# Loading and norming two heads first, and no weight product between the first head's scores

## The chip, the cores and the metric

The kernel runs on one core of a Trainium2 chip. Its time is device microseconds (us) of one execution. Three runs of the kernel before gave 1234.19 us as the median (1233.05 to 1234.97). One further execution was taken by the hardware profiler and took 1230.67 us, with a span of 1228.6 us from the first to the last instruction.

The engines are PE (matrix products), DVE (vector), ACT (scalar, with the exponentials), POOL (GpSimd) and SP, which here issues nearly all DMAs. Each works through its own instructions in order and waits for the others by semaphores.

## The reference

Four batches of attention with 12 heads, 448 rows and head width 64, on normed queries and keys, are followed by two dense blocks. All arrays are float32, except the weights of the dense blocks, which come as float64.

```
rmsnorm(x, g) = x / sqrt(mean(x*x, -1) + 1e-6) * g
scores = (1/8) * rmsnorm(q, g_q) @ rmsnorm(k, g_k).T
attn = softmax(scores);  x = attn @ v            # heads side by side: [1792, 768]
x = relu(x @ moe_w_in)**2 @ moe_w_out            # 768 -> 2048 -> 768
out = (((x @ w1) * (x @ w2)) @ w3) @ moe2_w_out  # 768 -> 1024 -> 1024 -> 768
```

The kernel uses that the last two products need no value between them: it forms W3O = w3 @ moe2_w_out once, at the start, and multiplies by that.

## The kernel before, in words

**Precision.** A product is made of three matmuls: each operand is split into a high part, which the matmul takes without loss, and a low part (the rest), and `mm3` (L260) adds high by high, high by low and low by high. L262, L263 and L264 are these three.

**Weight units.** The weights arrive as `units`: 128 partitions by 384 or 512 columns. A unit in float64 passes five steps: a load by SP (L180) into one of four `raw64` buffers; `words` (L191), where ACT rescales the upper word (L194) and POOL, for one unit in three ACT (L198), takes 16 bits of the lower word (L200); `join` on DVE (L207) makes a float32 and frees the load's buffer; `split_hi` on ACT (L106) makes the high part, and `split_lo` (L114) the low part, on POOL for four units in five and on DVE for the fifth. `advance` (L240) runs these steps some units ahead of use. The first 18 units, counted here from 0, belong to W3O: unit 0 (w3), 1 to 4 (wo), 5 (w3), 6 to 17 (wo). Unit 18 is the w3 unit of the second row of W3O, and from there on no wo unit is needed.

**W3O.** `gen_w3o` (L272) makes W3O in 8 rows of 48 matmuls, 384 in all. It and, for a batch later, `gen_moe` are generators: `fill(n)` (L649) lets the current one issue about n matmuls between stages of the attention. W3O's matmuls are recorded between the stages of heads 0 to 12, the dense blocks of batch 0 between those of heads 13 to 24, and so on.

**Heads.** `load_group` (L390) loads queries and keys of four heads for the norms, `load_head` the transposed queries of one head, `load_v` its values. `group_prep` (L438) squares them on ACT (L451), sums on DVE (L453), and makes 1/rms (L428 to L435, two steps of it on ACT); `sums` and `norm` of the first group are called in parts. `head_prep` (L475) scales the keys on POOL (L481), splits them (L108, L114: `khl`) and splits the queries (L492, L497). `stage_k` transposes the keys on PE (L509: `kv`) and copies them (`kt`). `stage_qk` makes the scores of two of a head's four 112-row chunks (L525, L526: `sc`, two PSUM buffers) and their maxima (L527, L528: `nb`). `stage_exp` takes the exponentials on ACT (L544: `p`). `stage_t` transposes the probabilities on PE (L571: `pt`), `stage_v` multiplies them by the values (L623).

**The order.** The program records instructions in the order of the loop at the end (L678). A scheduling layer then sets the order on each engine: it may place an instruction ahead of earlier ones that it expects to be still waiting. On the chip each engine keeps that order.

Of the kernel before, what the change touches and what calls it, by code (L numbers as in the profile page):

```python
# [29 lines left out]
def attention_moe_kernel(  # L30
# [15 lines left out]
    nc = tc.nc  # L46
    B, P, H, C, D = q_nat.shape
    S = P * C
    NH = B * H
    GH = 4  # L50
# [120 lines left out]
    def is64(i):  # L171
        return units[i][0].dtype != F32

    def load_next():
        i = pos["load"]
        src = units[i][0]
        n = src.shape[-1]
        if is64(i):
            t = t3.tile([128, 512, 2], U32, name="raw64", tag="raw64", bufs=4)
            nc.sync.dma_start(out=t[:, :n, :], in_=src.bitcast(U32).rearrange("p (n t) -> p n t", t=2))  # L180
        else:
            t = rawp.tile([128, 512], F32, name="raw", tag="raw")
            nc.sync.dma_start(out=t[:, :n], in_=src)
        raws[i] = t
        pos["load"] += 1

    def load_to(i):
        while pos["load"] <= min(i, NU - 1) and is64(pos["load"]):
            load_next()
# [200 lines left out]
    def load_group(g):  # L390
        if not (0 <= g < NH // GH):
            return
        b, h0 = divmod(g * GH, H)
        qn = t1.tile([P, GH, C, D], F32, name="qn", tag="qn")
        kn = t2.tile([P, GH, C, D], F32, name="kn", tag="kn")
        if g == 0:
            nc.sync.dma_start(out=kn[:, 0:1], in_=k_nat[0, :, 0:1])
            load_head(0)
            nc.sync.dma_start(out=qn[:, 0:1], in_=q_nat[0, :, 0:1])
            load_to(0)  # L400
            nc.sync.dma_start(out=kn[:, 1:], in_=k_nat[0, :, 1:GH])
            nc.sync.dma_start(out=qn[:, 1:], in_=q_nat[0, :, 1:GH])
            load_to(1)
        else:
            nc.sync.dma_start(out=kn, in_=k_nat[b, :, h0:h0 + GH])
            nc.sync.dma_start(out=qn, in_=q_nat[b, :, h0:h0 + GH])
        grp[g] = [qn, kn, None, None]

    def load_head(h):
        if not (0 <= h < NH):  # L410
            return
        b, hh = divmod(h, H)
        t = t2.tile([128, S], F32, name="qt", tag="qt")
        nc.sync.dma_start(out=t, in_=q_t[b, hh])
        qts[h] = t
# [9 lines left out]
    def rsqrt(y, x):  # L425
        t = small.tile([P, 2, GH * C], F32, name="nt", tag="nt")
        t = t[:, :x.shape[1], :x.shape[2]]
        nc.vector.tensor_scalar(  # L428
            out=y.bitcast(I32), in0=x.bitcast(I32), scalar1=-0.5, scalar2=1597463007.0, op0=ALU.mult, op1=ALU.add
        )  # L430
        nc.vector.tensor_tensor(out=t, in0=y, in1=y, op=ALU.mult)
        nc.vector.tensor_tensor(out=t, in0=t, in1=x, op=ALU.mult)
        nc.scalar.activation(out=t, in_=t, func=AF.Ln)
        nc.scalar.activation(out=t, in_=t, func=AF.Exp, scale=-0.5)
        ins = nc.vector.tensor_tensor(out=y, in0=t, in1=y, op=ALU.mult)  # L435
        return ins.ins

    def group_prep(g):  # L438
        if not (0 <= g < NH // GH):
            return  # L440
        qn, kn = grp[g][:2]
        n = GH * C
        if g == 0:
            sq = hlp.tile([128, 1024], F32, name="sq", tag="hl")[:P].rearrange("p (h c d) -> p h c d", h=GH, c=C)
        else:
            sq = qn
        ss = small.tile([P, 2, n], F32, name="ss", tag="ss")
        rr = grp[g][2] = t2.tile([P, 2, n], F32, name="rr", tag="rr")

        def sums(i, x, sq, a, b):  # L450
            nc.scalar.activation(out=sq[:, a:b], in_=x[:, a:b], func=AF.Square)  # L451
            t = sq[:, a:b].rearrange("p h c d -> p (h c) d")
            nc.vector.tensor_reduce(out=ss[:, i, a * C:b * C], in_=t, axis=AX.X, op=ALU.add)  # L453

        def norm(i, j, a, b):
            s = ss[:, i:j, a * C:b * C]
            nc.vector.tensor_scalar(out=s, in0=s, scalar1=1.0 / D, scalar2=1e-6, op0=ALU.mult, op1=ALU.add)
            return rsqrt(rr[:, i:j, a * C:b * C], s)

        if g == 0:  # L460
            sums(1, kn, sq, 0, 1)
            first.enter_context(tc.issue_after(norm(1, 2, 0, 1)))
            head_prep(0)
            stage_k(0)
            sums(0, qn, qn, 0, 1)
            norm(0, 1, 0, 1)
            sums(1, kn, sq, 1, GH)
            sums(0, qn, qn, 1, GH)
            norm(0, 2, 1, GH)
        else:  # L470
            sums(0, qn, qn, 0, GH)
            sums(1, kn, sq, 0, GH)
            norm(0, 2, 0, GH)

    def head_prep(h):  # L475
        if not (0 <= h < NH):
            return
        g, i = divmod(h, GH)
        _, kn, rr, _ = grp[g]
        kx = t1.tile([P, C, D], F32, name="kx", tag="kx")  # L480
        nc.gpsimd.tensor_tensor(  # L481
            out=kx, in0=kn[:, i], in1=rr[:, 1, i * C:(i + 1) * C].unsqueeze(2).to_broadcast([P, C, D]), op=ALU.mult
        )
        khl = t2.tile([P, C, 2 * D], F32R, name="khl", tag="khl")
        copy_on(KHI_ENG[h // H], khl[:, :, :D], kx)
        sub_on(KLO_ENG[h // H], khl[:, :, D:], kx, khl[:, :, :D].bitcast(F32))
        qt = qts.pop(h)
        qh = t2.tile([128, S], F32R, name="qh", tag="qh")
        ql = t2.tile([128, S], F32R, name="ql", tag="ql")
        qe = QHI_ENG[h // H]  # L490
        if qe == "a":
            nc.scalar.activation(out=qh, in_=qt, func=AF.Copy, scale=gg[:, 0:1])  # L492
        else:
            ENGS[qe].tensor_scalar(
                out=qh, in0=qt, scalar1=gg[:, 0:1], scalar2=1.0, op0=ALU.mult, op1=ALU.mult
            )
        nc.vector.scalar_tensor_tensor(  # L497
            out=ql, in0=qt, scalar=gg[:, 0:1], in1=qh.bitcast(F32), op0=ALU.mult, op1=ALU.subtract
        )
        heads[h] = dict(khl=khl, qh=qh, ql=ql, rq=rr[:, 0, i * C:(i + 1) * C], p=[None] * C, pt={}, lo=[])  # L500

    def stage_k(h):
        if not (0 <= h < NH):
            return
        d = heads[h]
        khl = d.pop("khl")
        ps = ps_kv.tile([128, 512], F32R, name="kv", tag="kv")
        for c in range(C):
            nc.tensor.transpose(ps[:, c * P:(c + 1) * P], khl[:, c, :], ident_r)  # L509
        kt = t2.tile([128, S], F32R, name="kt", tag="kt")  # L510
        copy_on("a", kt, ps[:, :S].bitcast(F32))
        d["kt"] = kt
# [133 lines left out]
    def start_fill(gen, total):  # L646
        state.update(gen=gen, credit=0.0, left=total)

    def fill(n):  # L649
        state["credit"] += n  # L650
        while state["gen"] is not None and state["credit"] > 0:
            try:
                k = next(state["gen"])
                state["credit"] -= k
                state["left"] -= k
            except StopIteration:
                state["gen"] = None

    MOE = 3 * (NFC * KX + 2 * NE * KF + 2 * NJ * KX + NE * NIC)
    W3O = 3 * 2 * NIC * NIC  # L660
# [1 line left out]
    nc.scalar.preload_act_table_set("natural_log_exp_and_others")  # L662
    nc.sync.dma_start(out=g_sb, in_=g_in)
    load_group(0)
    load_head(1)
    make_identity(nc, ident)
    nc.vector.tensor_copy(out=ident_r, in_=ident)
    nc.vector.scalar_tensor_tensor(
        out=gg, in0=g_sb[:, 0:1], scalar=float(D) ** -0.5, in1=g_sb[:, 1:2], op0=ALU.mult, op1=ALU.mult
    )  # L670
    first = ExitStack()
    group_prep(0)
    load_head(2)
    head_prep(1)
    load_v(0)
    start_fill(gen_w3o(), W3O)
    first.close()
    for h in range(NH + 1):  # L678
        n = W3O / ((H + 1) * 6) if h <= H else MOE / (H * 6)
        load_head(h + 3)  # L680
        load_v(h + 1)
        if h % GH == 0:
            load_group(h // GH + 1)
        stage_qk(h, 0)
        fill(n)
        stage_exp(h, 0)
        if h % H != 1:
            stage_x(h - 2)
        stage_t(h - 1, 0)
        stage_t(h - 1, 1)  # L690
        fill(n)
        stage_lo(h - 1)
        if h < NH:
            v_prep(h)
        fill(n)
        stage_k(h + 1)
        stage_t(h - 1, 2)
        stage_t(h - 1, 3)
        fill(n)
        stage_lo(h - 1)  # L700
        stage_qk(h, 1)
        fill(n)
        stage_exp(h, 1)
        fill(n)
        stage_v(h - 1)
        if h % GH == 1:
            group_prep(h // GH + 1)
        head_prep(h + 2)
        if h and h % H == 0:
            fill(1e9)  # L710
            stage_x(h - 1)
            start_fill(gen_moe(h // H - 1), MOE)
# [57 lines left out]
```

## Time and profile before

| | |
|---|---|
| median of three runs | 1234.19 us |
| profiled execution | 1230.67 us, span 1228.6 us |
| PE busy | 1162.9 us, 95% of the span |
| ACT, DVE, POOL busy | 732.0, 689.0, 781.5 us |
| PE waits, largest | scores for the exponentials (15.6 us), transposes for a DMA of the probabilities (10.4 us), the first transposes for the start (9.7 us) |
| granted PE clock | 0.989 of 2.4 GHz in the mean |

Since PE is busy 95% of the span, the time is PE's work and the 66 us in which PE does nothing. Of a stretch, one reads first how busy PE is, then which wait ends last there.

### The profile page before, as it was taken

To read this page: it belongs to the slowest core of one execution; us is meant where nothing else is said; L and a number is where in the kernel's file an instruction comes from. 1 tells how busy PE (TensorE), PEld (TensorE's weight loads), DVE (VectorE), ACT (ScalarE), POOL (GpSimd) and SP (SyncE) were. 2 spreads that over 40 slices of the span, in tenths; PEclk is the share of its full clock that TensorE was granted. 3 is DMA by queue.
4 is the path that set the end of the run, shared out by engine and by line. 5 is a ranking of instruction groups with operands and counts; after the bars stand their busy time and mean duration, and the time that the engine had idled before them with its cause. 6 is when DMAs were issued, how large, how long until landed. Compare 5 with 4: busy or idle time off the path is not lost.

```text
span 1228.6 us, 18882 instructions
## 1 busy us (share of the span) xinstructions
PE 1162.9 (95%) x6192; PEld 1050.8 (86%) x6192; DVE 689.0 (56%) x1230; ACT 732.0 (60%) x1581; POOL 781.5 (64%) x772
## 2 busy tenths in 40 slices
PE   4798999997988899999999999999999999999998
PEld 3587888886877799998998999999999999999998
DVE  5798888759978773556566554645655421012100
ACT  6898877767657565656646556656555544443442
POOL 5884425665676664756776664846766556678673
PEclk9799999999999999999999999999999999999999
DMA  7785457888788865545545455444543443333342
GB/s 224 246 256 158 146 148 237 271 290 251 256 254 261 245 192 172 146 131 150 159 114 167 134 168 164 140 133 136 153 123 114 138 138 114 110 113 103 104 125 75
DMA packets 111346, 207.63 MB, mean 169 GB/s; under 512 B 12208, under 2 KB 66704, under 8 KB 111248
## 3 DMA queue, kind: packets, MB, share of 16 engines
q1 hardware_dynamic: 107792, 200.92, 54.2%
q10 hardware_dynamic: 3456, 5.51, 1.2%
q8 instruction: 49, 0.80, 0.3%
q14 instruction: 49, 0.40, 0.1%
HBM read 149.95 MB, written 27.53 MB: 144 GB/s over the span
## 4 chain that ended last, share of the span: by engine, by line
PE 69%; DMA 10%; DVE 8%; ACT 5%; POOL 4%; issue 3%; SPq 1%; DVEq 0%; POOLq 0%; ACTq 0%
PE mm L262 19%; PE mm L263 19%; PE mm L264 19%; PE pt L571 4%; PE kv L623 3%; DMA raw<-w_out 2%; PE sc L525 2%; DMA raw<-w 2%; DMA pw<-p 2%; PE sc L526 2%; ACT p L544 2%; DMA raw<-w_in 2%; DVE nb L527 1%; POOL hl L114 1%; DVE raw L207 1%
## 5 line engine op out<-in xcount | busy, mean ns | idle before, releaser
L114 POOL TENSOR_TENSOR hl<-raw,hl 128x384 fp32r<-128x384 f32 (+1 forms) x383 | 446.3, 1169 | 261.3 <-ACT hl L106 250.8
L106 ACT ACTIVATE hl<-raw 128x384 fp32r<-128x384 f32 (+1 forms) x416 | 233.6, 564 | 148.8 <-PE mm L264 86.4
L262 PE MATMUL mm<-x,hl 128*128 128x448 f32 (+1 forms) x832 | 309.6, 372 | 1.4 <-DVE gf L334 1.4
L263 PE MATMUL mm<-x,hl 128*128 128x448 f32 (+1 forms) x832 | 305.9, 368 | 4.5 <-POOL x L114 4.4
L264 PE MATMUL mm<-x,hl 128*128 128x448 f32 (+1 forms) x832 | 304.9, 366 | 3.4 <-DVE hl L114 1.9
L263 PE MATMUL mm<-act,hl 128*128 128x448 f32 (+1 forms) x640 | 235.8, 368 | 3.2 <-POOL act L114 2.3
L262 PE MATMUL mm<-act,hl 128*128 128x448 f32 (+1 forms) x640 | 238.1, 372 | 0.0
L264 PE MATMUL mm<-act,hl 128*128 128x448 f32 (+1 forms) x640 | 234.5, 367 | 0.7 <-DVE hl L114 0.7
L544 ACT ACTIVATE p<-sc,nb,rr 112x448 f32<-112x448 f32 x192 | 137.5, 720 | 76.6 <-DVE nb L528 74.4
L263 PEld LDWEIGHTS mm<-x,hl 128*128 128x128 f32 x832 | 157.6, 189 | 19.2 <-POOL x L114 7.1
L264 PEld LDWEIGHTS mm<-x,hl 128*128 128x128 f32 x832 | 157.7, 189 | 17.2 <-DVE hl L114 2.3
L262 PEld LDWEIGHTS mm<-x,hl 128*128 128x128 f32 x832 | 157.8, 190 | 15.1 <-DVE gf L334 1.8
L527 DVE TENSOR_REDUCE nb<-sc 112x1 f32<-112x448 f32 x192 | 113.4, 615 | 40.3 <-PE sc L526 38.6
L263 PEld LDWEIGHTS mm<-act,hl 128*128 128x128 f32 x640 | 121.7, 190 | 14.6 <-POOL act L114 4.0
L264 PEld LDWEIGHTS mm<-act,hl 128*128 128x128 f32 x640 | 121.7, 190 | 10.7 <-DVE hl L114 1.1
L262 PEld LDWEIGHTS mm<-act,hl 128*128 128x128 f32 x640 | 121.7, 190 | 9.7
L114 DVE TENSOR_TENSOR ptr<-pt,ptr 128x448 fp32r<-128x448 f32 x144 | 86.8, 619 | 72.8 <-ACT ptr L106 72.0
L200 POOL TENSOR_SCALAR raw<-raw 128x384 uint32<-128x384 uint16 (+1 forms) x110 | 81.2, 739 | 64.5 <-DMA raw<-w_in 23.8
L207 DVE SCALAR_TENSOR_TENSOR raw<-raw 128x384 uint32<-128x384 uint32 (+1 forms) x120 | 82.7, 694 | 42.8 <-POOL hl L114 28.5
L114 POOL TENSOR_TENSOR act<-gf,act 128x448 fp32r<-128x448 f32 x80 | 97.1, 1214 | 7.6 <-ACT act L106 3.4
L194 ACT ACTIVATE raw<-raw 128x384 f32<-128x384 f32 (+1 forms) x120 | 70.6, 599 | 50.8 <-DMA raw<-w 17.6
L334 DVE TENSOR_TENSOR gf<-mm,r 128x448 f32<-128x448 f32 x64 | 39.8, 621 | 96.0 <-ACT r L330 95.4
(84 smaller groups left out, 1578.6 us busy)
## 6 DMA issues: line engine op xcount, KB each, us to landing
pw<-p SPq DMA_DIRECT2D x72, 392.0 KB, 4.3
raw<-f_in SPq DMA_DIRECT2D x96, 192.0 KB, 2.4
raw<-f_out SPq DMA_DIRECT2D x72, 256.0 KB, 2.7
raw<-f SPq DMA_DIRECT2D x96, 192.0 KB, 2.4
raw<-w_in SPq DMA_DIRECT2D x32, 384.0 KB, 4.5
raw<-w_out SPq DMA_DIRECT2D x24, 512.0 KB, 5.9
raw<-w SPq DMA_DIRECT2D x32, 384.0 KB, 5.0
raw<-w3o SPq DMA_DIRECT2D x48, 256.0 KB, 2.8
```

What stands on the lines that cost most here:

```text
L106: nc.scalar.activation(out=out, in_=in_, func=AF.Copy)
L114: e.tensor_tensor(out=out, in0=in0, in1=in1, op=ALU.subtract)
L194: nc.scalar.activation(out=hi, in_=hi, func=AF.Prelu, scale=2.0**-112, alpha=-(2.0**32))
L200: nc.gpsimd.tensor_scalar(out=t[:, :n, 0], in0=low, scalar1=2.0**-13, scalar2=2.0**-14 - 0.5, op0=ALU.mult, op1=ALU.add)
L207: nc.vector.scalar_tensor_tensor(out=f[:, :n].bitcast(U32), in0=t[:, :n, 1], scalar=3, in1=t[:, :n, 0], op0=ALU.logical_shift_left, op1=AL ...
L262: nc.tensor.matmul(ps, w[:, 0, wk, :], x[0], start=(i == 0), stop=False)
L263: nc.tensor.matmul(ps, w[:, 0, wk, :], x[1], start=False, stop=False)
L264: nc.tensor.matmul(ps, w[:, 1, wk, :], x[0], start=False, stop=(i == last))
L334: nc.vector.tensor_tensor(out=gf, in0=ps, in1=r, op=ALU.mult)
L527: nc.vector.tensor_reduce(out=nb[:, j:j + 1], in_=o[j], axis=AX.X, op=ALU.max, negate=True)
L544: nc.scalar.activation(out=p, in_=o[j], func=AF.Exp, scale=d["rq"][:, c:c + 1], bias=nb[:, j:j + 1], accum_out=sm[:, i, c:c + 1],)
L571: nc.tensor.transpose(to[:kn, c * P:(c + 1) * P], d["p"][c][:, k0:k0 + kn], one)
```

## The change

`load_group(0)` loads the keys and queries of heads 0 and 1 first, then those of heads 2 and 3 (before: of head 0, then of heads 1 to 3). The transposed queries of head 1 are loaded ahead of W3O's second unit, and units 2 and 3 of W3O are loaded ahead of the transposed queries of head 2. Norms and preparation follow the same halves: head 1 is prepared before heads 2 and 3 are normed. In head 0's turn the first four `fill` calls are left out, and n for heads 0 to 12 becomes 384/74 = 5.19 (before 384/78 = 4.92), so that W3O's total stays.

```diff
         if g == 0:
-            nc.sync.dma_start(out=kn[:, 0:1], in_=k_nat[0, :, 0:1])
+            nc.sync.dma_start(out=kn[:, 0:2], in_=k_nat[0, :, 0:2])
             load_head(0)
-            nc.sync.dma_start(out=qn[:, 0:1], in_=q_nat[0, :, 0:1])
+            nc.sync.dma_start(out=qn[:, 0:2], in_=q_nat[0, :, 0:2])
             load_to(0)
-            nc.sync.dma_start(out=kn[:, 1:], in_=k_nat[0, :, 1:GH])
-            nc.sync.dma_start(out=qn[:, 1:], in_=q_nat[0, :, 1:GH])
+            load_head(1)
             load_to(1)
+            nc.sync.dma_start(out=kn[:, 2:], in_=k_nat[0, :, 2:GH])
+            nc.sync.dma_start(out=qn[:, 2:], in_=q_nat[0, :, 2:GH])
+            load_to(3)
...
         if g == 0:
-            sums(1, kn, sq, 0, 1)
-            first.enter_context(tc.issue_after(norm(1, 2, 0, 1)))
+            sums(1, kn, sq, 0, 2)
+            first.enter_context(tc.issue_after(norm(1, 2, 0, 2)))
             head_prep(0)
             stage_k(0)
-            sums(0, qn, qn, 0, 1)
-            norm(0, 1, 0, 1)
-            sums(1, kn, sq, 1, GH)
-            sums(0, qn, qn, 1, GH)
-            norm(0, 2, 1, GH)
+            sums(0, qn, qn, 0, 2)
+            norm(0, 1, 0, 2)
+            head_prep(1)
+            sums(1, kn, sq, 2, GH)
+            sums(0, qn, qn, 2, GH)
+            norm(0, 2, 2, GH)
...
     load_group(0)
-    load_head(1)
...
     load_head(2)
-    head_prep(1)
     load_v(0)
...
-        n = W3O / ((H + 1) * 6) if h <= H else MOE / (H * 6)
+        n = W3O / (H * 6 + 2) if h <= H else MOE / (H * 6)
...
         stage_qk(h, 0)
-        fill(n)
+        if h:
+            fill(n)
...
```

The same `if h:` stands before the three next `fill(n)`. On every engine the order changes in about the first sixth of the program; on PE the orders are the same again from the 875th of 6194 matmuls on. In the rows below line numbers of the changed program are 2 or 3 higher.

**POOL, from its first work on head 0.** `raw_119` is unit 0, `raw_123` unit 1, `raw_129` unit 3; `khl` are the split keys of a head. Before:

```order
L481 TENSOR_TENSOR kx<-kn,rr 112x256
L200 TENSOR_SCALAR raw_119<-raw_119 128x512
L108 TENSOR_SCALAR khl<-kx 112x4x64
L114 TENSOR_TENSOR khl<-kx,khl 112x4x64
L200 TENSOR_SCALAR raw_123<-raw_123 128x384
L114 TENSOR_TENSOR hl<-raw,hl 128x512
L114 TENSOR_TENSOR x<-raw,x 128x384
L481 TENSOR_TENSOR kx<-kn,rr 112x256
L114 TENSOR_TENSOR vhl<-v,vhl 128x4x64
L108 TENSOR_SCALAR khl<-kx 112x4x64
L114 TENSOR_TENSOR vhl<-v,vhl 128x4x64
L114 TENSOR_TENSOR khl<-kx,khl 112x4x64
```

And now:

```order
L484 TENSOR_TENSOR kx<-kn,rr 112x256
L200 TENSOR_SCALAR raw_119<-raw_119 128x512
L108 TENSOR_SCALAR khl<-kx 112x4x64
L200 TENSOR_SCALAR raw_123<-raw_123 128x384
L114 TENSOR_TENSOR khl<-kx,khl 112x4x64
L484 TENSOR_TENSOR kx<-kn,rr 112x256
L108 TENSOR_SCALAR khl<-kx 112x4x64
L114 TENSOR_TENSOR khl<-kx,khl 112x4x64
L114 TENSOR_TENSOR hl<-raw,hl 128x512
L200 TENSOR_SCALAR raw_129<-raw_129 128x384
L114 TENSOR_TENSOR x<-raw,x 128x384
L114 TENSOR_TENSOR vhl<-v,vhl 128x4x64
```

Head 1's keys (the second `kx` and the two `khl` behind it) move ahead of W3O's first low parts, and the last step on head 0's keys moves behind a step on unit 1.

**SP's queue, from the first keys to the first loads behind the second group's queries.** `kn`, `qn` are the keys and queries for the norms (256 columns a head), `qt` the transposed queries, `raw_216` and `raw_218` before and `raw_127` and `raw_129` now are units 2 and 3. Before:

```order
L397 DMA kn<-k_nat 112x256
L414 DMA qt<-q_t 128x448
L399 DMA qn<-q_nat 112x256
L180 DMA raw_119<-w3t 128x1024
L401 DMA kn<-k_nat 112x768
L402 DMA qn<-q_nat 112x768
L180 DMA raw_123<-wo 128x768
L414 DMA qt<-q_t 128x448 x2
L422 DMA v<-v_in 128x256 x2
L405 DMA kn<-k_nat 112x1024
L414 DMA qt<-q_t 128x448
L406 DMA qn<-q_nat 112x1024
```

And now, from the same place:

```order
L397 DMA kn<-k_nat 112x512
L416 DMA qt<-q_t 128x448
L399 DMA qn<-q_nat 112x512
L180 DMA raw_119<-w3t 128x1024
L416 DMA qt<-q_t 128x448
L180 DMA raw_123<-wo 128x768
L403 DMA kn<-k_nat 112x512
L404 DMA qn<-q_nat 112x512
L180 DMA raw_127<-wo 128x768
L180 DMA raw_129<-wo 128x768
L416 DMA qt<-q_t 128x448
L424 DMA v<-v_in 128x256
```

Units 2 and 3 are in the queue before the second head pair's queries and all values; before, they stood behind the whole second group.

**PE, around the end of W3O's first row.** `mm_562` before and `mm_649` now is the first half of the second row, whose L264 is the first to need the low part of unit 18; `sc` are scores of head 2, `kv` the transposed keys of head 3. Before:

```order
L262 MATMUL mm_393<-x2_462,hl_279 128x384
L263 MATMUL mm_393<-x2_462,hl_279 128x384
L264 MATMUL mm_393<-x2_462,hl_279 128x384
L262 MATMUL mm_393<-x2_491,hl_279 128x384
L263 MATMUL mm_393<-x2_491,hl_279 128x384
L264 MATMUL mm_393<-x2_491,hl_279 128x384
L262 MATMUL mm_562<-x_240,hl_503 128x384
L263 MATMUL mm_562<-x_240,hl_503 128x384
L623 MATMUL kv_604<-pte_545,vhl_313 128x448
L571 MATMUL pt_679<-ident_103,p_468 128x112
L264 MATMUL mm_562<-x_240,hl_503 128x384
```

And now:

```order
L574 MATMUL pt_639<-ident_103,p_535 128x112
L262 MATMUL mm_441<-x2_529,hl_303 128x384
L263 MATMUL mm_441<-x2_529,hl_303 128x384
L264 MATMUL mm_441<-x2_529,hl_303 128x384
L512 MATMUL kv_676<-ident_r_104,khl_583 128x112 x4
L262 MATMUL mm_649<-x_264,hl_549 128x384
L263 MATMUL mm_649<-x_264,hl_549 128x384
L262 MATMUL mm_736<-act_386,hl_549 128x384
L263 MATMUL mm_736<-act_386,hl_549 128x384
L264 MATMUL mm_649<-x_264,hl_549 128x384
```

Work on later heads and on the row's other half has moved ahead of that L264: from the program's start to it, PE has 104 matmuls before and 119 now (4 more for scores, 4 and 5 more for transposes of keys and of probabilities, 2 more of W3O).

## Rows read from the trace of the kernel before

**Rows 1.** Busy time by stretch: length, each engine's busy us (instructions), PE clock, DMA

```profile
0.00:24.00 24.00, 7.79 (x27) 5.38 (x27) 13.93 (x35) 13.23 (x28) 13.26 (x24) 1.00 0.77 235
24.00:57.00 33.00, 23.74 (x77) 17.61 (x77) 23.32 (x38) 27.12 (x60) 27.18 (x27) 0.79 0.75 242
57.00:92.00 35.00, 34.92 (x214) 31.49 (x215) 32.53 (x58) 33.18 (x72) 28.65 (x32) 1.00 0.80 248
92.00:120.00 28.00, 24.18 (x145) 20.67 (x143) 23.65 (x48) 23.93 (x54) 14.87 (x20) 1.00 0.57 168
120.00:192.00 72.00, 66.17 (x406) 59.77 (x406) 60.67 (x126) 55.40 (x128) 29.42 (x38) 1.00 0.53 155
```

**Rows 2.** PE's waits from 0 to 120 us: us in total, times, longest

```profile
PE sc L525 <- ACT p L544: 4.8, 4, 2.2
PE mm L263 <- POOL x L114: 3.1, 4, 1.3
PE mm L263 <- POOL act L114: 2.3, 3, 1.5
```

**Rows 3.** SP's queue in order of time: start, length, line, DMA

```profile
2.12 0.43 SPq L399 DMA_DIRECT2D qn<-q_nat  x1
...
8.26 0.43 SPq L405 DMA_DIRECT2D kn<-k_nat  x1
...
14.34 1.38 SPq L180 DMA_DIRECT2D raw<-wo  x3
...
25.19 2.70 SPq L180 DMA_DIRECT2D raw<-wo  x3
```

**Rows 4.** DMAs issued at 2.12, 8.26 and 14.34: size, us to landing

```profile
qn<-q_nat SPq DMA_DIRECT2D x1, 112.0 KB, 2.7
...
kn<-k_nat SPq DMA_DIRECT2D x1, 448.0 KB, 6.4
...
raw<-wo SPq DMA_DIRECT2D x1, 384.0 KB, 5.3
```

**Rows 5.** The start in order of time: start, length, instruction, wait ahead of it

```profile
3.75 0.42 ACT L451 ACTIVATE sq<-kn 112x256 f32<-112x256 f32 x1 [1.74 <-DMA kn<-k_nat]
...
8.68 0.72 POOL L114 TENSOR_TENSOR khl<-kx,khl 112x256 fp32r<-112x256 f32 x1
...
9.70 0.71 PE L509 MATMUL kv<-ident_r,khl 112*128 112x112 f32 x4 [9.70 <-DVE ident_r L667]
...
11.12 0.53 POOL L200 TENSOR_SCALAR raw<-raw 128x384 uint32<-128x384 uint16 x1 [1.71 <-DMA raw<-wo]
...
16.61 0.72 ACT L544 ACTIVATE p<-sc,nb,rr 112x448 f32<-112x448 f32 x1 [0.53 <-DVE nb L528]
```

**Rows 6.** From unit 2 to the first use of unit 18, in order of time

```profile
23.49 0.55 ACT L194 ACTIVATE raw<-raw 128x384 f32<-128x384 f32 x1
...
26.78 0.73 ACT L544 ACTIVATE p<-sc,nb,rr 112x448 f32<-112x448 f32 x1
...
32.23 1.34 POOL L114 TENSOR_TENSOR hl<-raw,hl 128x512 fp32r<-128x512 f32 x1 [1.46 <-ACT hl L106]
...
40.11 0.81 POOL L200 TENSOR_SCALAR raw<-raw 128x384 uint32<-128x384 uint16 x1 [1.21 <-DMA raw<-wo]
...
55.21 1.78 POOL L114 TENSOR_TENSOR hl<-raw,hl 128x512 fp32r<-128x512 f32 x1
...
57.04 0.44 PE L264 MATMUL mm<-x,hl 128*128 128x384 f32 x1 [1.39 <-POOL hl L114]
...
57.22 0.74 POOL L114 TENSOR_TENSOR vhl<-v,vhl 128x256 fp32r<-128x256 f32 x1 [0.23 <-DVE vhl L110]
...
62.19 0.99 POOL L557 TENSOR_SCALAR rsw<-rs 112x512 f32<-112x512 f32 x1 [0.42 <-DVE rs L555]
```

**Rows 7.** POOL from 24 to 57 us by group: count, busy, mean ns, idle ahead

```profile
L114 POOL TENSOR_TENSOR x<-raw,x 128x384 fp32r<-128x384 f32 x6 | 7.6, 1268 | 0.8 <-ACT x L106 0.5
...
L200 POOL TENSOR_SCALAR raw<-raw 128x384 uint32<-128x384 uint16 x10 | 6.7, 667 | 3.1 <-DMA raw<-wo 2.4
```

More of the change, by code (lines that the diff above doesn't have):

```diff
@@ L690, in attention_moe_kernel @@
         stage_t(h - 1, 1)
-        fill(n)
+        if h:
+            fill(n)
         stage_lo(h - 1)
@@ L694, in attention_moe_kernel @@
             v_prep(h)
-        fill(n)
+        if h:
+            fill(n)
         stage_k(h + 1)
@@ L698, in attention_moe_kernel @@
         stage_t(h - 1, 3)
-        fill(n)
+        if h:
+            fill(n)
         stage_lo(h - 1)
```

## The prediction

> **What bounds the kernel now.** I read the busy times by stretch first [rows 1]. From 57 us on PE is full (34.92 of 35 us). Up to 24 us it is busy 7.79 us, and from 24 to 57 us 23.74 of 33. So the start is lost to waiting, and only there do the two programs differ much. Then PE's waits in it [rows 2]: for exponentials 4.8 us, for low parts of W3O's operands from POOL 3.1 and 2.3. The waits name two chains: head 0's and head 1's way to their exponentials, and the supply of W3O's units. The order of time [rows 5, 6] gives the links. Unit 2 reaches ACT at 23.49 us, its load having been issued at 14.34 and landed 5.3 later, at 19.6 [rows 3, 4]. The next loads leave at 25.19, when joins free `raw64` buffers. At 40.11 POOL waits for a load, and at 57.04 PE waits for the last time for a low part, that of unit 18. From 24 to 57 us POOL and ACT are the busiest engines (27.18 and 27.12 of 33 us), so the units' pace is set by POOL and by the loop of four buffers.
>
> **The first loads.** Between the landing of the first queries at 4.8 us (2.12 + 2.7) and of the second group's keys at 14.7 (8.26 + 6.4) the queue moved 2720 KB, so 276 KB/us [rows 3, 4]. The first keys are 112 KB more now: 0.4 us later than 3.75 [rows 5]. Square and sum take twice the columns; each lengthens by less than its 0.42, I take 0.2. Head 0's norm is thus about 0.8 us late. On how a transfer's time grows, the Trainium skill (DMA: Bandwidth & Descriptors, Anatomy of one DMA) gives 2.0 us plus the bytes at 436 KB/us. By it the 112 KB more would cost 0.3 us instead of 0.4, and the sum would not differ by more than 0.1; the row of 448 KB in 6.4 us shows the queue behind it, not the fixed part.
>
> **Head 0 comes later.** On POOL the last step on its keys now stands behind unit 1's word step, which waits for its load. Before, that load was in at 11.0 (the wait of [rows 5] ends at 11.12); now 224 KB fewer are ahead of it, so 10.3. Add 0.53 for the step and 0.72 for the keys: the transposes start at about 11.7 instead of 9.70, 2.0 late. Part of this is hidden, for at 16.61 the first exponential came at the end of DVE's work on heads 1 to 3, half of which moves behind it. Bounds: 0 to 2.0 late. I take the middle, 1.1: 17.7 us.
>
> **Head 1 no longer blocks PE.** Before, PE held head 0's second score matmuls behind head 1's keys, and its last exponential came at 26.78 [rows 6], 10.2 us after the first. Now head 1's keys are on POOL right behind head 0's, done by about 13.5 us. What stands in their place ahead of those scores is W3O's work with units 1 and 2, six matmuls, the fifth of which waits for POOL's low part of unit 2 (about 19). Behind it come four score matmuls, two maxima and head 2's transposes. Bounds for the last exponential: no gain (26.8) and the lateness taken from the old distance, with the keys' waits of some 6 us gone (22). I take 24.4, 2.4 early.
>
> **Units 2 and 3 come sooner.** They land at 4.8 + (2624 - 448)/276 = 12.7 and 14.1 instead of 19.6 and after, so their steps fill ACT, POOL and DVE while head 0 waits. The gain is at most 6.9 us; at least it is -1.1, if everything goes on being queued behind head 0's exponentials. For unit 5 I follow ACT: from the last exponential of head 0 at 24.4 (0.6) eight instructions of 0.5 to 1.05 us (5.3) and its own split (0.6) give 30.9, against 32.23 for POOL's low part [rows 6], 1.3 early. The load for which POOL waits at 40.11 follows the join of unit 8, and this the buffers freed earlier; the 1.21 us of waiting [rows 6] mostly go. So I take 2.0 us as the lead of the supply at 40 us, nearest to the row at 32.23 and that wait together. From there POOL is full and keeps it.
>
> **What stands ahead of unit 18 now.** On POOL the second head's values (0.74) and the first pair's sums (0.99) move from behind its low part to ahead of it [rows 6]: 1.7 us. So PE's last such wait ends 2.0 - 1.7 = 0.3 early, at about 56.7. But PE has then done 119 matmuls instead of 104. At the pace of the full stretch, 34.92 us for 214 or 0.163 each [rows 1], these 15 are worth 2.4 us.
>
> **No fill in head 0, more later.** W3O keeps its 384 matmuls, and only their places move; n grows by 0.27 a call. Its cost is in the count just made, nothing more. If heads run ahead of W3O, W3O's units must be joined later, on a DVE that is busy 32.53 of 35 us: that is a rival below.
>
> **Sum.** -0.3 - 2.4 = -2.7 us at the start. From 57 to 192 us PE does nothing for 0.1 + 3.8 + 5.8 = 9.7 us [rows 1]; I leave this as it is, and behind 192 the orders are the same and shift as a whole. The profiled execution would go from 1230.67 to 1228.0 us (span 1225.9). The median of the runs is 3.5 above the profiled one, so I forecast 1231.5.
>
> **The rivals.**
>
> *Half a head is won.* At the 108th matmul of W3O PE has done 32 score matmuls instead of 28, half a head. If the heads' chain, not PE's work, paces the twelve heads from 57 to 192 us (11.2 us each), half a head is 5.6 us, with the 0.3 together 5.9: 1228.3. For it speaks that in that stretch DVE and ACT are over 90% busy at first; against it that PE is at 99.8%. Chance 0.19.
>
> *POOL and DVE get in each other's way.* The same word step took 0.53 us at 11.12 and 0.81 at 40.11, the same low part 1.34 at 32.23 and 1.78 at 55.21 [rows 5, 6]: where DVE works beside it, POOL takes longer. If the ramp becomes denser, ten word steps go from 0.667 to 0.81 (1.4 us) and six low parts of 1.268 lengthen by a third (2.5) [rows 7]. That is 3.9 lost against 2.7 won: 1235.4, no change that can be told. The Trainium skill (SBUF — State Buffer, Who interferes with whom) states a rule of that kind: a vector instruction with two SBUF inputs and a GpSimd instruction that reads SBUF lock each other out for the whole instruction. The lengths here agree with it, and by it the ramp would give nothing; but the same pairs of steps overlap before and after, so I think it less likely. Chance 0.13.
>
> *DVE becomes the bound.* With heads half a head ahead of W3O from 57 us on, their maxima and low parts come on top of the joins, on a DVE that has 2.5 us free in 35. Past that PE waits for it as it does from 92 to 120 us, 3.8 of 28 us, 14%. From 57 to 92 that is 4.8 us; the 15 matmuls ahead then count nothing, only the 0.3 stays: 1234.19 + 4.5 = 1238.7, slower. For it: PE's idle time begins right where the busy time of DVE had been highest. Against it: the work ahead was done in the start, where DVE has room (23.32 of 33 us). Chance 0.18.
>
> **How the numbers follow.** The forecast has the rest, 0.50, with a range of its own from 1229 to 1233.5. About 0.2%, or 2.5 us, is what a measurement of this kernel can tell from no change, so the forecast lies just beyond that edge: of its 0.50, 0.30 fall on faster. Faster 0.30 + 0.19 = 0.49; same 0.20 + 0.13 = 0.33; slower 0.18. The range goes from below the half-head rival (some of the supply's bound of 6.9 us beside it) to near the DVE rival: 1226.0 to 1238.0.
>
> **What would show it.** Right: the first exponential at 17 to 19 us, the last of head 0 by 25; units 2 and 3 on ACT before 16; no wait of POOL for a load near 40; PE full from about 56; the same idle 9 to 10 us up to 192, and all later stretches earlier by one amount. Wrong: POOL's low part of unit 5 no earlier than 32; PE's idle time between 57 and 120 above 7 us with DVE full; or a start that gains over 5 us by 92 us, which would say that the heads were the pace.

## The result: slower, 1240.45 us against 1234.19

The changed kernel takes 1240.45 us (median of 5 runs, 1237.64 to 1241.06), the kernel before 1234.19 (median of 5 runs, 1233.05 to 1234.97). The ratio is 1.0057, with a 95% interval from 1.0037 to 1.0077, so 4.6 to 9.5 us slower. The forecast was 1231.5 with a range up to 1238.0: the sign was wrong and the time fell outside. The profiled execution took 1237.64 us, 6.97 more than the one before; its span is 1235.9.

The stretches of the changed kernel (length, then busy us and instructions of PE, PEld, DVE, ACT, POOL, then PE's granted clock, DMA share, GB/s) answer to [rows 1]:

```profile
0.00:24.00 24.00, 6.95 (x23) 5.27 (x24) 11.78 (x33) 12.87 (x28) 13.49 (x23) 1.00 0.85 263
24.00:57.00 33.00, 21.84 (x89) 15.75 (x89) 21.78 (x39) 27.55 (x60) 25.77 (x29) 0.90 0.64 206
57.00:92.00 35.00, 33.29 (x191) 29.38 (x190) 30.22 (x56) 30.24 (x67) 25.40 (x30) 0.95 0.79 246
92.00:120.00 28.00, 24.93 (x155) 22.11 (x153) 25.36 (x47) 26.27 (x58) 17.69 (x21) 1.00 0.52 152
120.00:192.00 72.00, 65.28 (x391) 59.10 (x392) 56.73 (x118) 52.10 (x118) 26.57 (x35) 0.98 0.48 143
```

Add up PE's matmuls and set them beside [rows 1]; a matmul that lies across an edge counts in both stretches. At 57 us there are 112 instead of 104: the start did gain, 8 matmuls or 1.3 us at 0.163 each. At 92 us there are 303 instead of 318, so the sign has turned within one stretch. At 192 us there are 849 instead of 869, 20 behind or 3.3 us. The stretch from 57 to 92 was the full one before (34.92 us busy at clock 1.00). Now PE stands idle for 1.7 of it, and the granted clock is 0.95, which is worth another 1.75 us (0.05 x 35). Note that no other engine is fuller than before there: DVE, ACT and POOL all do less.

The rest of the loss comes behind 192 us. The changed kernel first, then the kernel before, same columns:

```profile
192.00:300.00 108.00, 97.03 (x529) 85.77 (x527) 85.47 (x154) 74.98 (x166) 63.76 (x69) 1.00 0.85 268
...
420.00:620.00 200.00, 196.12 (x1067) 178.46 (x1066) 113.99 (x199) 120.54 (x266) 128.19 (x121) 0.99 0.55 162
```

```profile
192.00:300.00 108.00, 100.50 (x535) 89.62 (x536) 82.47 (x150) 75.79 (x166) 62.52 (x70) 0.98 0.81 263
...
420.00:620.00 200.00, 198.84 (x1085) 182.10 (x1084) 116.67 (x200) 122.36 (x268) 132.36 (x123) 1.00 0.54 158
```

From 900 us on PE is full in both (325 of 325 us) and nothing changes any more. The trace gives the same by place in the program: PE's 875th matmul, from which on both orders are the same, starts at 193.7 us before and at 198.7 now, 5.0 late, and the span ends 7.2 late. So all of the loss is decided while heads run beside W3O and the first layers behind it, some two thirds of it before 200 us.

PE's waits up to 120 us (us in total, times, longest) answer to [rows 2]:

```profile
PE mm L263 <- POOL x L114: 7.4, 6, 2.4
PE pt L574 <- DVE ptr L114: 2.8, 4, 1.0
PE mm L263 <- DVE act L114: 1.8, 2, 1.0
PE mm L263 <- POOL act L114: 1.7, 4, 0.9
...
PE sc L528 <- ACT p L547: 0.9, 1, 0.9
```

The wait for exponentials went from 4.8 to 0.9 us, as the edit meant; the wait for W3O's low parts from POOL went from 3.1 and 2.3 to 7.4 and 1.7 and took its place.

The start in order of time, as [rows 5], then from unit 2 on, as [rows 6]:

```profile
4.12 0.63 ACT L453 ACTIVATE sq<-kn 112x512 f32<-112x512 f32 x1 [2.11 <-DMA kn<-k_nat]
...
6.77 0.63 ACT L453 ACTIVATE qn<-qn 112x512 f32<-112x512 f32 x1 [1.28 <-DMA qn<-q_nat]
...
7.77 0.17 DVE L437 TENSOR_TENSOR rr<-nt,rr 112x8 f32<-112x8 f32 x1 [1.49 <-ACT nt L436]
...
12.16 0.54 POOL L200 TENSOR_SCALAR raw<-raw 128x384 uint32<-128x384 uint16 x1 [1.72 <-DMA raw<-wo]
...
12.78 1.11 POOL L114 TENSOR_TENSOR khl<-kx,khl 112x256 fp32r<-112x256 f32 x1
...
13.95 0.73 PE L512 MATMUL kv<-ident_r,khl 112*128 112x112 f32 x4 [13.95 <-POOL khl L114]
...
15.68 0.55 ACT L194 ACTIVATE raw<-raw 128x384 f32<-128x384 f32 x1
...
19.75 0.71 ACT L547 ACTIVATE p<-sc,nb,rr 112x448 f32<-112x448 f32 x1
...
27.53 0.72 ACT L547 ACTIVATE p<-sc,nb,rr 112x448 f32<-112x448 f32 x1
...
33.57 1.31 POOL L114 TENSOR_TENSOR hl<-raw,hl 128x512 fp32r<-128x512 f32 x1 [3.71 <-ACT hl L106]
...
40.08 0.54 POOL L200 TENSOR_SCALAR raw<-raw 128x384 uint32<-128x384 uint16 x1 [0.17 <-DMA raw<-wo]
...
54.09 1.54 POOL L560 TENSOR_SCALAR rsw<-rs 112x512 f32<-112x512 f32 x1 [0.35 <-DVE rs L558]
...
56.65 0.44 PE L263 MATMUL mm<-x,hl 128*128 128x384 f32 x1 [2.38 <-POOL x L114]
...
57.42 1.80 POOL L114 TENSOR_TENSOR hl<-raw,hl 128x512 fp32r<-128x512 f32 x1
...
59.27 0.69 PE L264 MATMUL mm<-x,hl 128*128 128x384 f32 x1
```

Head 0's transposes begin 4.25 us later than before, its first exponential 3.1, its last 0.75. Unit 5's low part is 1.3 late, unit 18's 2.2. Behind the wait of 2.38 us that ends at 56.65 the granted clock goes to the lower of its two levels, 1.2 instead of 2.4 GHz (PE's matmuls are in the second group of numbers):

```profile
54.00:56.00 2.00, 0.27 (x2) 0.02 (x1) 1.68 (x4) 2.00 (x4) 1.91 (x2) 1.00 0.83 238
56.00:58.00 2.00, 1.35 (x7) 1.27 (x8) 0.62 (x2) 2.00 (x5) 1.84 (x3) 0.76 0.80 213
58.00:60.00 2.00, 1.95 (x6) 1.44 (x6) 1.97 (x6) 1.13 (x3) 1.87 (x2) 0.50 0.83 231
60.00:62.00 2.00, 2.00 (x11) 2.00 (x11) 2.00 (x5) 0.12 (x1) 1.07 (x1) 0.88 0.47 182
```

Six and eleven matmuls in 2 us, where before 15 and 15 stood. The same happens once more before 192 us, behind this matmul, which waited 2.62 us for DVE:

```profile
121.20 0.57 PE L615 MATMUL kv<-ident,rsw 112*128 112x112 f32 x4 [2.62 <-DVE xf L634]
```

### The profile page after: what moved, and what is told of

Same layout as the page of the kernel before. It is cut to its first block, busy times and chain, and to the rows that moved or that the text cites. A ratio compares the mean times of both kernels' runs of the same rounds, so it can differ in the third digit from the quotient of the medians.

```text
span 1235.9 us, 18880 instructions
## 1 busy us (share of the span) xinstructions
PE 1162.9 (94%) x6192; PEld 1049.9 (85%) x6192; DVE 687.4 (56%) x1230; ACT 732.4 (59%) x1581; POOL 778.0 (63%) x772
## 3 DMA queue, kind: packets, MB, share of 16 engines
HBM read 149.95 MB, written 27.53 MB: 144 GB/s over the span
## 4 chain that ended last, share of the span: by engine, by line
PE 65%; DMA 11%; DVE 9%; POOL 6%; ACT 5%; issue 4%; SPq 1%; DVEq 0%; POOLq 0%; ACTq 0%
PE mm L262 18%; PE mm L263 18%; PE mm L264 18%; PE pt L574 3%; PE kv L626 3%; DMA pw<-p 3%; DMA raw<-w_in 2%; PE sc L528 2%; POOL hl L114 2%; PE sc L529 2%; DVE nb L530 2%; ACT p L547 2%; DVE raw L207 2%; POOL raw L200 1%; POOL x L114 1%
## 5 line engine op out<-in xcount | busy, mean ns | idle before, releaser
L264 PE MATMUL mm<-x,hl 128*128 128x448 f32 (+1 forms) x832 | 305.9, 368 | 3.5 <-DVE hl L114 2.3
L264 PE MATMUL mm<-act,hl 128*128 128x448 f32 (+1 forms) x640 | 233.5, 365 | 0.0
L263 PEld LDWEIGHTS mm<-x,hl 128*128 128x128 f32 x832 | 157.8, 190 | 22.4 <-POOL x L114 10.4
L264 PEld LDWEIGHTS mm<-x,hl 128*128 128x128 f32 x832 | 157.8, 190 | 18.3 <-POOL hl L114 2.9
L263 PEld LDWEIGHTS mm<-act,hl 128*128 128x128 f32 x640 | 121.2, 189 | 14.6 <-POOL act L114 3.1
L264 PEld LDWEIGHTS mm<-act,hl 128*128 128x128 f32 x640 | 121.0, 189 | 9.8 <-DVE hl L114 0.2
L207 DVE SCALAR_TENSOR_TENSOR raw<-raw 128x384 uint32<-128x384 uint32 (+1 forms) x120 | 86.1, 721 | 49.8 <-POOL hl L114 38.3
```

The source lines that it names most:

```text
L207: nc.vector.scalar_tensor_tensor(out=f[:, :n].bitcast(U32), in0=t[:, :n, 1], scalar=3, in1=t[:, :n, 0], op0=ALU.logical_shift_left, op1=AL ...
L263: nc.tensor.matmul(ps, w[:, 0, wk, :], x[1], start=False, stop=False)
L264: nc.tensor.matmul(ps, w[:, 1, wk, :], x[0], start=False, stop=(i == last))
```

## The experiments

All times are ratios to the kernel before on the same chip, 5 rounds each; 0.1% is 1.2 us. The change has three parts: the pairs (keys and queries of heads 0 and 1 loaded and normed together), the early units (W3O's units 2 and 3), and the fills (none between head 0's scores, and n raised from 4.92 to 5.19). In the table, "exp." is the start of head 0's first and last exponential, "idle" is PE's idle time from 57 to 192 us, and "lost to the clock" is (1 - granted clock) x 135 us, an estimate from the clock's row, in which one step of the rounding is worth 1.35 us and half clock counts while PE is idle too. These two columns and the exponentials come from one profiled execution of each kernel.

| kernel | ratio (95% interval) | us | exp. | idle | lost to the clock |
|---|---|---|---|---|---|
| before | 1 | 0 | 16.6, 26.8 | 9.7 | 0 |
| pairs + units | 1.0007 (0.9992 to 1.0023) | +0.9 | 19.0, 28.2 | 7.3 | 4.1 |
| density alone | 1.0008 (0.9994 to 1.0023) | +1.0 | 16.6, 26.8 | 9.5 | 4.1 |
| lump | 1.0010 (0.9997 to 1.0023) | +1.2 | 18.8, 26.6 | 11.3 | 2.7 |
| catch-up | 1.0022 (1.0010 to 1.0034) | +2.7 | 18.9, 26.7 | 11.7 | 5.4 |
| pairs | 1.0039 (1.0023 to 1.0055) | +4.8 | 20.9, 31.2 | 10.8 | 4.1 |
| half | 1.0048 (1.0031 to 1.0066) | +5.9 | 18.9, 28.3 | 11.0 | 4.1 |
| changed kernel | 1.0057 (1.0037 to 1.0077) | +7.0 | 19.8, 27.5 | 11.5 | 4.1 |
| units | 1.0077 (1.0057 to 1.0097) | +9.5 | 22.0, 29.9 | 12.0 | 5.4 |
| more | 1.0084 (1.0064 to 1.0103) | +10.4 | 19.0, 28.4 | 17.0 | 5.4 |
| changed, keys on DVE | 1.0100 (1.0082 to 1.0118) | +12.3 | 20.4, 27.9 | 16.2 | 6.8 |
| pairs + fills | 1.0112 (1.0094 to 1.0130) | +13.8 | 19.5, 29.9 | 16.4 | 6.8 |
| fills | 1.0128 (1.0109 to 1.0147) | +15.8 | 17.3, 27.4 | 15.8 | 8.1 |
| units + fills | 1.0143 (1.0121 to 1.0166) | +17.6 | 21.7, 30.0 | 16.9 | 5.4 |

**The parts alone.** Each was done on the kernel before:

```
pairs:  the diff without load_to(3), n and the four "if h"
units:  -            load_to(1)
        +            load_to(3)
fills:  -        n = W3O / ((H + 1) * 6) if h <= H else MOE / (H * 6)
        +        n = W3O / (H * 6 + 2) if h <= H else MOE / (H * 6)
        +        if h:      (around the first four fills)
```

> Only the pairs: keys and queries of heads 0 and 1 loaded, normed and prepared first, head 1's transposed queries ahead of unit 1; units 2 and 3 and the fills as before. Theory A (the late start of head 0 is what costs): first exponential near 19.7 us as in the changed kernel, 4 to 7 us slower than before. Theory B (the fills and with them the order from 57 to 192 us cost): within 2.5 us of before. Theory C (the two units crowd the first loads): within 2.5 us of before, first exponential near 17.5.

> Only units 2 and 3 loaded sooner, behind the first group and ahead of head 1's transposed queries. Theory A: head 0's first exponential within 0.5 us of 16.6, time within 2.5 us of before or up to 4 us faster, since the supply of units has its lead without the late head. Theory B: the same, within 2.5 us. Theory C: 3 to 7 us slower.

> Only the fills: none of the first four in head 0, n of 5.19 for heads 0 to 12. Theory A: within 2.5 us of before. Theory B: 4 to 7 us slower, lost between 57 and 192 us with the start unchanged up to 24 us. Theory C: within 2.5 us of before.

> Units 2 and 3 sooner and the fills changed, no pairs. Theory A: within 2.5 us of before, or faster by up to 4 us. Theory B: 4 to 7 us slower. Theory C: 3 to 7 us slower.

Pairs alone cost 4.8 us, units alone 9.5, fills alone 15.8, units with fills 17.6. All of them slow the kernel. Theory A fits the pairs, whose last exponential of head 0 comes at 31.2. Theory B fits the fills by the place of their loss, though not by its size (4 to 7 us were expected), and none of the three had as much for the units or for units with fills. And no theory of single parts fits the whole, which costs only 7.0. The stretch from 57 to 192 us of the fills alone, whose exponentials are late by only 0.65 us:

```profile
57.00:192.00 135.00, 119.17 (x689) 107.07 (x690) 110.90 (x206) 102.32 (x227) 68.41 (x83) 0.94 0.56 166
```

PE stands idle for 15.8 us there instead of 9.7, and runs at 0.94 of the clock, with 689 matmuls done. The late start is thus not what the fills cost. What PE waits for in that stretch (us in total, times, longest):

```profile
PE sc L525 <- ACT p L544: 8.2, 8, 2.8
PE kv L623 <- DVE ptr L114: 4.5, 2, 3.8
PE mm L263 <- POOL x L114: 3.1, 1, 3.1
```

These are waits of the later heads, for their exponentials and their transposed probabilities; only the third is one of W3O's.

**Two parts at a time, and the density of fills.** The other two pairs of parts, the kernel before with the raised n alone, and the changed kernel with one step moved off POOL:

```
pairs + units:  the diff without n and the four "if h"
pairs + fills:  the diff without load_to(3)
density:        the line of n alone, on the kernel before
keys on DVE:    sub_on(KLO_ENG[h // H] if h else "v", khl, ...)   on the changed kernel
```

> Pairs and early units together, with the fills as before. Sum theory (each part costs what it costs alone): 5.4 + 9.2 = about 14.6 us above before. Cover theory (PE's loss is its waits outside of head 0, each over 2 us followed by half clock, and what decides is how much work stands ready beside a head's exponentials; pairs make head 1's keys ready and the fills in head 0 then have nothing to replace): start late as with the units alone, first exponential at 20 to 22 us, time 5 to 10 above before, and PE's idle time between matmul 119 and 874 at most 3 us above before's 8.6.

> Pairs without the early units, with no fill in head 0's scores: the changed kernel with its two early loads taken back. Sum theory: 5.4 + 15.5 = about 21 us above before. Cover theory: the pairs alone give back what the missing fills take, so about as the changed kernel, 4 to 8 above before, and the early units are worth within 2 us of nothing. If the early units are what the changed kernel lives on (they cost alone, and supply W3O without head 0's fills), it is 12 or more above before.

> The kernel before with only the number of matmuls per fill raised from 4.92 to 5.19; head 0 keeps its four fills. If the missing fills in head 0 cost the 15.5 us of the third part, this is within 2 us of before. If the denser fills of heads 1 to 12 cost it, it is 8 or more above. If any other order than the one before costs (waits of PE that fall anew), it is 3 to 10 above, with new waits of PE between 57 and 192 us and half clock behind the longest of them.

> The changed kernel with one step moved: the low part of head 0's keys goes from POOL, where it stands behind the word step that waits for unit 1, to DVE. Late-start theory (3 us of the loss are head 0's late keys and pass through to the end): transposes 2 to 3 us earlier, first exponential near 17.5, time 2 to 4 us less than the changed kernel. If the loss arises behind 57 us alone: first exponential earlier, time within 1.5 us of the changed kernel.

The sum theory fell: pairs and units together cost 0.9 us, no change that can be told, where 14.6 was the sum. The cover theory fell too: it had 5 to 10 us for that kernel, and 4 to 8 for pairs with fills, which cost 13.8. The third case of pairs with fills did hold (12 or more without the early units): beside the other two parts, the early units take 6.8 us off. What holds in all four settings is the sign of the third part: with the fills taken out of head 0 the kernel loses 15.8 us (alone), 9.0 (beside the pairs), 8.1 (beside the units) and 6.1 (beside both, which is the changed kernel). And it is not n alone: raised by itself it costs 1.0, within the measurement. The stretch of pairs with units:

```profile
57.00:192.00 135.00, 127.71 (x753) 113.94 (x751) 114.21 (x227) 111.56 (x248) 70.83 (x87) 0.97 0.59 178
```

PE is idle for less than before here, 7.3 us, although head 0's first exponential came 2.4 us later; part of its busy time is at half clock, and it does 753 matmuls instead of 762. The kernel before:

```profile
57.00:192.00 135.00, 125.26 (x762) 111.92 (x762) 116.85 (x230) 112.51 (x253) 72.94 (x89) 1.00 0.61 182
```

With the keys on DVE, head 0's transposes start at 12.04 instead of 13.95, as was expected. But the first exponential is at 20.4, later than the changed kernel's 19.75, since DVE reaches head 0's maxima later; and the kernel loses another 5 us, in the same stretch:

```profile
57.00:192.00 135.00, 118.82 (x684) 105.80 (x685) 109.59 (x205) 104.24 (x229) 71.94 (x85) 0.95 0.57 168
```

So an earlier step in the start did not reach the end here.

**Where W3O stands.** If the missing fills cost, is it because head 0's waits stay empty, or because from then on W3O stands some 20 matmuls behind the heads? In the lump the first four fills only keep their credit, which the fifth spends behind the second scores. In the half, they place half. In "more", all six of head 0 place 8. All three have pairs and units.

```
lump:  +        if h:
                    fill(n)
       +        else:
       +            state["credit"] += n
half:           fill(n if h else n / 2)           (n = W3O / (H * 6 + 4); in the lump n is as before)
more:           n = 8 if h == 0 else (W3O - 48) / (H * 6) if h <= H else MOE / (H * 6)
```

> Pairs and early units, the same number of W3O matmuls in head 0 as with the fills, but none between its scores: the first four fills' matmuls come in one lump with the fifth, behind the second scores. Count theory (the missing fills cost because PE enters head 1 some 20 W3O matmuls behind, and has to fit them where it is full): within 2.5 us of pairs and units with the fills, so 0 to 3 above before. Cover theory (the fills cost because the scores' waits in head 0 stay empty): as the changed kernel, 5 to 9 above before, the last exponential of head 0 no later than the changed kernel's 27.5.

> Pairs and early units, the first four fills with half their matmuls. If the loss follows the number of matmuls missing: about half of the way from pairs and units with fills (+1) to the changed kernel (+7), so 3 to 5 above before. If the loss comes from any shift of W3O against the heads: anywhere from 2 to 12 above, with no relation to the half.

> Pairs and early units, with 8 matmuls instead of 4.9 in each of head 0's six fills and 4.67 in the later ones. Count theory: the work ahead is won, 1 to 3 us below pairs and units with the usual fills, so 0 to 2 below before, if W3O's units are there. Supply theory (in head 0 PE waits for W3O's low parts, and more fills only block its scores): 2 to 6 us above before, the last exponential of head 0 beyond 30.

The lump costs 1.2 us, with an interval that ends at 2.8, below the 4.6 where that of the changed kernel begins. Its program, too, has no fill between head 0's scores, and PE's first 76 matmuls are in the same order as the changed kernel's (in both, the scheduling layer places six matmuls of W3O between the first scores and the second): only where the 20 matmuls go differs. So it is not the cover in head 0. The count theory in its simple form fell as well, for more matmuls ahead cost 10.4 instead of gaining; the half does not decide about it, since its 5.9 (3.8 to 8.1) leaves room for half of the way. The supply theory did not hold for head 0 either. Up to 35 us PE's waits for POOL's low parts are the same with more fills as with the usual ones (1.2 and 0.2 us), and the last exponential is at 28.4, where the theory had it beyond 30; the kernel loses behind 57 us:

```profile
57.00:192.00 135.00, 117.97 (x696) 106.17 (x697) 107.52 (x202) 102.90 (x227) 71.23 (x85) 0.96 0.56 165
```

**Catching up in head 1.** The last run leaves head 0 as in the changed kernel and returns to the usual position before head 2:

```
-        n = W3O / (H * 6 + 2) if h <= H else MOE / (H * 6)
+        n = W3O / ((H + 1) * 6) if h <= H else MOE / (H * 6)
+        if h == 1:
+            n = n * 10 / 6
```

> The changed kernel, no fill between head 0's scores, but head 1's six fills take the 20 matmuls that head 0 left (8.2 each), and from head 2 on W3O stands against the heads as with the usual fills. Phase theory (the loss arises from head 2 on, where W3O falls otherwise against the heads' waits): as with the lump in head 0, 0 to 3 us above before. Cover theory, or supply (head 0's and head 1's units come too late either way): 5 to 9 above before, as the changed kernel. A fill of 8 in head 1 that blocks its scores would add up to 3 to either.

It costs 2.7 us (1.2 to 4.2), as the phase theory had it: most of the loss is gone, and what is left is more than nothing. Two different ways of giving the 20 matmuls back, and by their medians both take 4 to 6 of the changed kernel's 7 us away. With pairs and units in place, what decides is thus the position of W3O against the heads from head 1 or 2 on. A position behind costs, one ahead costs as well, and the usual one is the best of those tried.

This rests on the ratios. The profiles, one execution each, do not show it: there PE's 875th matmul is 5.0 us late in the changed kernel, 4.8 with the lump, 6.0 with the catch-up and 2.6 with pairs and units. The catch-up's profiled execution took 1237.01 us, one of the slower of its twelve (1231.98 to 1238.89).

The table's last two columns say where the large losses are. Together they are 9.7 us before, 11 to 17 in the kernels up to 9.5 us slower, and 22 to 24 in the five that lose 10 us or more. Below that they do not rank the kernels: the catch-up has 17.1 for 2.7 us, the pairs 14.9 for 4.8. Every one of the other kernels has stretches at half clock between 57 and 192 us, the kernel before has none.

## Why the prediction was wrong

**The first loads.** The keys' 0.4 us were right (the square at 4.12 instead of 3.75). The queries were not counted: their 224 KB landed 4.6 us after their issue, not 2.7, and their square stands on ACT ahead of the two steps of the keys' norm. The norm's last step began at 7.77, 1.7 us later than before (6.06), where 0.8 was expected.

**Head 0 comes later.** Here a rate was taken for a landing. Unit 1 was expected at 10.3, since fewer bytes were ahead of it; it landed at about 12.1, later than before, with the keys on POOL behind it, whose low part took 1.11 us where 0.72 was counted. The transposes came at 13.95 instead of 11.7 and the first exponential at 19.75 instead of 17.7: 3.1 late, outside the bounds of 0 to 2.0. So the last one came at 27.53, not 24.4. Only the distance shrank, from 10.2 to 7.8 us.

**Units 2 and 3.** They came sooner than before, but unit 2 landed 9.1 us after its issue at 5.33, so at 14.4 instead of 12.7, and was on ACT at 15.68. The supply's lead of 2.0 us never arose: unit 5's low part is at 33.57, 1.3 late where 1.3 early was said. It waited 3.71 us for ACT, whose next unit stood behind head 0's exponentials, as the lower bound had it. The wait for a load near 40 went, as expected, to 0.17.

**Unit 18.** Its low part starts 2.2 us later than before, at 57.42. The sums of the first pair did move ahead of it. PE's wait did end at 56.65 (56.7 was said), but the matmul that waited was another unit's, and unit 18's followed at 59.27.

**The start's sum** was forecast at 2.7 us, of which 1.3 are seen at 57 us. With pairs and units alone PE has 110 matmuls there by the same count, so the first two parts bring 6 of the 8. Where the forecast counted, at the L264 of unit 18, less is left: it is PE's 120th matmul now and starts at 59.27, and the 120th of the kernel before starts at 59.70. That is 0.4 us instead of 2.7.

**The step that failed** is one clause of the sum: "From 57 to 192 us PE does nothing for 0.1 + 3.8 + 5.8 = 9.7 us [rows 1]; I leave this as it is". The edit of which it said "Its cost is in the count just made, nothing more", no fill in head 0, moves W3O against the heads through all of that stretch, and the idle time there did not stay: it went from 9.7 to 11.5, and some 3 us lost to half clock came on top (0.05 x 35 + 0.02 x 72). By the trace PE goes from 0.4 us early at its 120th matmul to 5.0 late at its 875th, 5.4 us where the sum had none. The experiments show that, beside pairs and units, this part turns no change (+0.9) into +7.0, and that giving the 20 matmuls back takes most of it away. Behind the 875th matmul the shift was not one amount either, and it grew to 7.2: from 420 to 620 us PE is idle for 3.9 us instead of 1.2.

**The rivals.** Half a head won did not happen: at 92 us PE was behind. POOL and DVE in each other's way did not decide: POOL's low parts and word steps from 24 to 57 us are about as long as in [rows 7]:

```profile
L200 POOL TENSOR_SCALAR raw<-raw 128x384 uint32<-128x384 uint16 (+1 forms) x11 | 7.6, 688 | 1.0 <-DMA raw<-wo 0.2
...
L114 POOL TENSOR_TENSOR x<-raw,x 128x384 fp32r<-128x384 f32 x5 | 5.9, 1189 | 0.3
```

On head 0's path they may have cost the 0.4 us by which the low part at 12.78 was longer than counted; no run tests it. And "where DVE works beside it, POOL takes longer" read [rows 5] and [rows 6] too widely, for DVE worked beside the short word step at 11.12 as well. Beside that step it ran a sum of squares, beside the long one at 40.11 a join, and beside the low part at 12.78 a join again (two lines of the kernel before, then one of the changed kernel):

```profile
11.16 0.94 DVE L453 TENSOR_REDUCE ss<-qn 112x12 f32<-112x768 f32 x1
...
39.97 0.55 DVE L207 SCALAR_TENSOR_TENSOR raw<-raw 128x384 uint32<-128x384 uint32 x1
```

```profile
12.75 0.56 DVE L207 SCALAR_TENSOR_TENSOR raw<-raw 128x384 uint32<-128x384 uint32 x1 [0.43 <-POOL raw L200]
```

The rival on DVE gave 1238.7 us, near the measured time, but for another reason: it wanted DVE full from 57 to 92 us, and DVE is busy for 30.22 us there instead of 32.53.

**What stays open.** Why a given position of W3O hits a given wait was not traced. The waits differ from kernel to kernel: from 57 to 192 us PE waits for POOL's low parts of W3O for 0.4 us with pairs and units, 2.4 in the changed kernel, 5.4 in the half and 5.6 with more fills, while the fills alone lose most to the heads' own waits, as shown above. What was shown is the sum of them. Why pairs alone or units alone cost 4.8 and 9.5 us and both together nothing was not settled. Their starts are late (first exponentials at 20.9 and 22.0), but so is that of both (19.0).

## What to carry to other kernels

Where an engine is nearly full beside two interleaved streams, as here, an edit ahead of that stretch can have two effects: the time it wins, and the new position of one stream against the other. Price the second from both sides, as an unknown of the size of the idle time already there, and never at nothing; then look for the cheapest way to keep the old position, as the lump does. And test the parts of an edit in pairs too: here each of three cost something alone, and only the set of all eight combinations showed which one did the harm.

## What the runs showed of the hardware that was not expected

A load's landing time grew with what was in flight. The queries' load issued at 2.12 us (224 KB; before, 112 KB in 2.7) and unit 2's issued at 5.33:

```profile
qn<-q_nat SPq DMA_DIRECT2D x1, 224.0 KB, 4.6
...
raw<-wo SPq DMA_DIRECT2D x1, 384.0 KB, 9.1
```

The 384 KB took 5.3 us when issued at 14.34 before [rows 4]. At 5.33 six of SP's earlier loads were still in flight, at 14.34 three. The total rate was higher at the same time (263 GB/s from 0 to 24 us against 235), so more bytes moved and these loads still came later. The fit that the prediction quotes from the Trainium skill (DMA: Bandwidth & Descriptors, Anatomy of one DMA) is stated there for DMAs that GpSimd issues, and these are SP's. SP's two issues at 5.33 were long as well (start, length, line, DMA), against 0.43 us for one at 2.12; what held them was not traced:

```profile
5.33 2.12 SPq L180 DMA_DIRECT2D raw<-wo  x2
```

And PE's granted clock fell to 0.50 right behind the waits of 2.38 and 2.62 us shown above, in a stretch in which it had been 1.00 throughout in the kernel before, and came back some 3 us later. By rows of 2 us this cost up to another 1.7 us behind each of the two waits (from 56 us on 0.24 x 2 + 0.50 x 2 + 0.12 x 2, from 120 us on 0.02 x 2 + 0.50 x 2 + 0.33 x 2).
